# Storing the output rows from SyncE's queue instead of ScalarE's in a fused attention and feed-forward kernel

## The chip, the cores and the metric

One core of one Trainium2 chip runs the whole program. The metric is the device time of one execution in microseconds. A core has a matrix engine (TensorE, PE in the profile), three engines for elementwise work (VectorE, DVE; ScalarE, ACT; GpSimd, POOL) and SyncE (SP), which in this kernel only issues DMAs. ACT and POOL can issue DMAs as well. Each engine takes its own instructions strictly in order.

## The reference

Inputs are q, k, v of shape 4 × 8 × 768 × 64 (batch, head, position, dimension) and the weights of a feed-forward layer. The attention has two kinds of keys under one softmax: the near positions, |i − j| < 16, and 24 summaries of blocks of 32 positions.

```python
k_sum = k.reshape(B, H, nb, block, D).max(axis=3)
v_sum = v.reshape(B, H, nb, block, D).mean(axis=3)
scores_l = scale * q @ k.T                      # kept where |i - j| < 16
scores_s = scale * q @ k_sum.T + log(block)
a = softmax(concat[scores_l, scores_s])
attn = a @ concat[v, v_sum]
x = attn.transpose(0, 2, 1, 3).reshape(3072, 512)
xn = x / sqrt(mean(x * x) + 1e-6) * rms_g
g = xn @ w_gate                                 # 512 -> 1536
out = (g * sigmoid(g) * (xn @ w_val)) @ w_out   # 1536 -> 512
```

The output is 3072 × 512 in float32, 6.29 MB.

## The kernel before, in words

The tokens are cut into 24 units of 128, six per batch. Attention runs unit by unit, all heads together. Units 0 to 5 (batch 0) go through steps whose names begin with su, in float32, and PE transposes their operands. Units 6 to 23 use operands that are split into a high and a low float16 part, and DMA transpositions turn them: kT of the keys (line 729), qT of the queries (`prep_q`, line 796), eT of the exponentials (`expo`, line 858), and, for every unit from 3 on, xT of the normalized attention output (`norm_b`, line 1111). All DMA transpositions are issued by SP; so are all loads.

The block summaries of batches 1 to 3 are made from pieces, hn, of k (the maximum, on DVE, line 682) and of v (the sum, on POOL, line 682). There are eight pieces of each per batch, loaded at line 666 into two buffers; ACT takes sums of squares of them (line 676), the folded results go to memory (`sum`, line 693), and `sum_scale` (line 699) lets PE add the squares up. `load_ks` (line 715) reads the summaries of k back as kr; `split_ks` (line 723) splits them on ACT into khl, which SP transposes into ksT (line 729).

Meanwhile the weights are loaded by SP in pieces of 1 MB (w_gate and w_val at line 554, w_out at line 560), decoded and split: lines 542 to 590 for w_gate and w_val into w_gv, lines 611 to 649 for w_out, where `row_o` (line 627) takes row sums on ACT.

The feed-forward layer runs over nine groups of tokens, of 384, 128, 256 and then six times 384. For each group and each of 12 slices f of the 1536 columns, `gate_val` (line 1258) multiplies xT with the slices of w_gate and w_val, and ACT and DVE form the product h (lines 1267 to 1270); for groups 5 to 8 `seven` (line 1190) does part of it with fewer products. `project` (line 1292) multiplies h with the slice of w_out and accumulates in three PSUM banks, acc, one for each 128 tokens. After the last slice ACT evicts each bank into a tile ob with two buffers (line 1297; the very last tile of the program uses another one, x), and the tile is stored as 256 KB (lines 1298 and 1299). There are 24 such stores. With `qout="a"` ACT's queue issues them, otherwise SP's.

The steps are written in one long list, which fixes the data flow. The order in which each engine issues its instructions is a second thing: a table, ORDER, holds for PE, ACT, DVE, POOL and SP a list of jumps over the instructions as the list produced them, and every engine follows its list. The tables also say where in its queue an engine meets a store or a transposition, and so what waits behind it.

Of the kernel before, what the change touches and what calls it, by code (L numbers as in the profile page):

```python
# [35 lines left out]
    e32a="a", e32b="v", ee="a", fill1="v", fill2="p", hh="a", hh0="a", hl="v", k32="a", ob="v", q32="a", qout="a",  # L36
# [114 lines left out]
0x22 36x2 -38x18 20 -21x8 13 -14x10 8x4 -7 -2 2 -2 13 4x2 -15x4 1 1 -4 1 27x3 -22 -7x2 5 20x2 1 -2 2x2 -23x2 -6x4 23  # L151
-34 33x4 -37 11x2 6 -7 -4 3x2 12 7 -21x3 18x8 -25 27 55 -48 47 -48 -14x3 1x8 2x4 43 1 12 -59 2 55 -16 1 13x3 -62x2 20
23 15x4 -56 -8 8 -2 -8x5 57x5 13 -14x4 -52 -15 75x6 -78 6 -7x2 5 -6x4 27 -17x6 -13x6 79x3 -75 -8 24 -8 63x6 -62 -8x6
-17x2 35x5 11x10 -21x2 19 -20x2 34x9 -25x7 18x6 6x4 8x7 30 -31 -16x2 -12 26 -27 24 29x4 -48 15x2 -28x4 54 -48x5 43 26x2
-28x2 33x2 -9x7 2x2 -37 11 -47x2 11x2 -13x3 10 -11x6 36 23 1x2 -3 -57 -6x2 4x8 10x6 7 -8 7 -8x3 5 -6 53 18 -19 -50x3
21x2 10 -11 23x2 -25 24x2 -51 53 3 -58x2 48x2 -28 27 -28 32 -5 -53 72 -50x2 36x2 -33x3 -8 7 -8x3 23 3 1x2 -3 -5 19
-11x3 8 -9x3 6 -7 -36x7 29x2 4x3 32x4 8x4 -12 -37x2 46 -12x2 -34x3 1 -8 36x2 -33 1 38 -9x2 22x2 -56x2 -10 9x2 35 -36x4
58 -59 31 -32 22 -18 -6 34 -5 4x3 -33 32 -39x2 43 -7x4 13 -26 -30x2 2 50 -51x3 36 -15 14 19 -10 -11x3 17 -36 -52 117x4
-35x4 3x2 10 -11x3 -8 -23 7 -8 7 -8x2 6x4 39 1 -2 1 -34 33x2 -35 5 -17 44x3 -47 15x2 5x3 -8x4 4x8 20 -8x2 6x2 -8x2 6 -7
6x4 -10 13x6 55 -56x4 9 -10 -24 23x4 47 -43x2 -26 25 -8 1x2 -3 14x4 -12x5 7 -8 7x2 -9x2 7x3 -44x3 63x4 6 -7x3 4x5 7 -17  # L160
8x2 -10 9 28x2 -71 40 -40x2 67 -68 1 -2 40 -40 -7 45 -6 5 -41 5 57 -64 34 -35x4 17 -17x4 24 -25 29 7 -8x5 26 -9 19x3
-41x2 1x5 11 21 -22 6 -7 6 -7x2 5 16 -17 -7 6x2 -8 7 64 -91 90x2 -92 24 66x6 -97x2 35x4 -16 15x12 -51 94 -45x7 -57 28
1x2 -3 78x8 16 -39x2 -74 73 36 -37x3 34x2 -36x4 32 -33 32x6 -38 37 -121 92x5 -15 14 -15 14x3 19x8 -27x7 20 3x2 -5 4x2
-104x5 99x4 -102x4 98 15 23x4 -54 10x5 58 -59 10x3 -13x2 -18 52x3 -38 10x2 -12 36x4 -29x2 -13x2 11x2 -129 115 12 24x13
-37 -14 13 -14 -114x2 2x2 -4x2 2x12 145 23 -24 23 -24 23x2 20x11 -56 55x2 -97x2 38 -39x5 34 55 -56 55x3 -94x4 32x3 62x2
-9x5 -60x2 16 45 -63 62 -63 62 -63 14x2 -16 15 -16 60 -46x2 44x2 17 -18x2 -65 64 15 -16x2 14x14 -79x6 30 -31x3 70x8 -36
-68 52 -53 23 -24 23x2 -25 24x2 -26 63x10 -73 313x8 16x19 -35x16 -265 283x5 6x6 -268 2 -3x2 1 1 -2 262x3 -264x2 3 -4 3
-22x8 10 4x2 -3 -4 5x2 3 -4 3 13 -18 3 -4 3 14x2 -4 -5x2 3 -4 5 228 -223 -7 2 3 -4 -4 3 -4 5x2 2 2 -3x2 1 -7x2 5 3 2
-42x2 37 -36 -3 2x2 -4 3 34 -8x2 6 -7 2 205 -200 -4 5 -6 5 -4 -3 5 -4 46 -4 5x2 -7 2 -3 5 -4 3 2 2x2 -7 2 3 -7 -52 4
-5x4 1x3 1 -2 1 3 -4 41 3 5 -4x2 -4 5 -3 2 -7 12 -61 2 -3 5 49 -54x2 2 -3 2x2 1 -2 1x4 5 -6 5x3 -8x4 4 34 -8x2 2x2 -4 5  # L170
3 2 -7x3 4x2 -5x2 3x20 89x2 -91x6 85 -86 85x2 -87x2 105 -106x2 127 -128 82 -83 102x4 -106x3 123 -124x2 124 -24x2 19x2
-124x3 149 -76x2 -76 75x2 44x2 -46 21 49 -27 -124x2 76x2 20x7 -57 2x3 51x2 43 -3 -68 25x2 93x5 5 -104x4 100x3 -103 -65
# [1167 lines left out]
```

## Time and profile before

| what | value |
|---|---|
| median of 3 runs | 706.21 us (702.89 to 707.88) |
| profiled execution | 708.47 us |
| its span | 706.6 us |
| mean granted clock of PE | 0.988 |
| PE busy | 676.8 us, 96% of the span |
| DVE, ACT, POOL busy | 540.8, 497.3, 221.4 us |
| SP's DMA queue, q1 | 239,172 packets, 84.78 MB |
| ACT's DMA queue, q10 (the stores alone) | 3,456 packets, 6.29 MB |

The profile is of one execution. Times within it count from the span's start. In a list of waits, "A <- B: 3.3, 1, 3.3" says that A waited for B 3.3 us in total, once, the longest 3.3 us. In a timeline an idle time of the engine ahead of an instruction stands in brackets with what ended it. The granted clock is a share of PE's full clock of 2.4 GHz. A row of SPq or ACTq is the issue of a DMA by that engine's sequencer, not its transfer.

### The profile page before, as it was taken

The numbers are of one execution on the slowest core, as the hardware profiler recorded it, in microseconds if no ns is written. First come the engines' busy times: TensorE is split into PE (matmuls) and PEld (weight loads), VectorE is DVE, ScalarE is ACT, GpSimd is POOL, SyncE is SP. The second block draws the span as 40 slices with busy tenths as digits, with TensorE's granted clock in tenths as the row PEclk, the third lists the DMA queues.
The fourth block names the chain that finished last, engine by engine and source line by source line (L and its number), as shares of the span: only waits on it lengthen the run. The fifth ranks groups of instructions, "written<-read, shape, count | busy, mean of one in ns | idle before, by whom it ended". The sixth has DMA issues, their size and how long they took to land.

```text
span 706.6 us, 16113 instructions
## 1 busy us (share of the span) xinstructions
PE 676.8 (96%) x5854; PEld 482.1 (68%) x5854; DVE 540.8 (77%) x1599; ACT 497.3 (70%) x1095; POOL 221.4 (31%) x321
## 2 busy tenths in 40 slices
PE   6998999887999999999999999999999999999997
PEld 4686666774556765655655566777988788878874
DVE  3898897766878865766999989999888877675542
ACT  3696785579988678747778687677888778834433
POOL 5564132450333344423125444251233213410000
PEclk9998999988999999999999999999999999999999
DMA  9999645455569698694677774563768444320001
GB/s 192 312 283 289 209 158 123 86 111 118 104 143 154 142 195 161 147 176 100 97 149 183 138 156 109 101 129 72 147 116 160 102 99 84 76 53 19 29 1 60
DMA packets 243859, 93.32 MB, mean 132 GB/s; under 512 B 227716, under 2 KB 227716, under 8 KB 243780
## 3 DMA queue, kind: packets, MB, share of 16 engines
q1 hardware_dynamic: 239172, 84.78, 56.3%
q10 hardware_dynamic: 3456, 6.29, 2.5%
q0 software_dynamic: 1152, 1.22, 0.8%
q8 instruction: 46, 0.75, 0.4%
q14 instruction: 33, 0.27, 0.1%
HBM read 50.45 MB, written 6.59 MB: 81 GB/s over the span
## 4 chain that ended last, share of the span: by engine, by line
PE 64%; DMA 12%; DVE 7%; ACT 6%; SPq 5%; issue 4%; POOL 2%; POOLq 0%; ACTq 0%; DVEq 0%
PE acc L1292 20%; PE gv L1190 17%; PE gv L1258 17%; DMA qT<-qs 4%; SPq L745 3%; PE att L834 3%; PE acc L1258 2%; PE att L875 2%; DMA eT<-ee 2%; DMA wo<-in_moe_w_val_dram 1%; DMA wo<-in_moe_w_gate_dram 1%; ACT junk L627 1%; SPq L554 1%; DMA hn<-in_k_dram 1%; POOL ee L436 1%
## 5 line engine op out<-in xcount | busy, mean ns | idle before, releaser
L1292 PE MATMUL acc<-wo,hhl 128*128 128x512 f16 x864 | 230.2, 381 | 0.3 <-ACT ob L1297 0.2
L1258 PE MATMUL gv<-xT,w_gv 128*128 128x384 f16 (+2 forms) x1296 | 218.7, 306 | 8.3 <-DVE th L1270 4.1
L1258 PEld LDWEIGHTS <-w_gv 128*128 128x128 f16 x1584 | 142.3, 99 | 80.4 <-issue 8.2
L1292 PEld LDWEIGHTS <-hhl 128*128 128x128 f16 x864 | 81.3, 98 | 61.8 <-issue 2.1
L436 POOL TENSOR_TENSOR ee<-sm,ee 128x256 f16<-128x256 f32 (+1 forms) x72 | 70.5, 991 | 154.7 <-ACT ee L431 132.0
L1190 PEld LDWEIGHTS <-w_gv 128*128 128x128 f16 x1008 | 87.3, 98 | 12.1 <-issue 1.5
L849 ACT ACTIVATE sm<-sm,mx,c 128x192 f32<-128x192 f32 x144 | 69.8, 537 | 1.9
L1190 PE MATMUL gv<-S,w_gv 128*128 128x192 f16 x504 | 65.7, 246 | 0.0
L1190 PE MATMUL gv<-xT,w_gv 128*128 128x192 f16 x504 | 54.6, 246 | 0.6 <-DVE R L1224 0.5
L838 DVE CUSTOM_DVE_ANT_0 sm<-att,mask 128x192 f32<-128x192 f32 x144 | 44.6, 352 | 9.3 <-PE att L834 6.2
L1190 PEld LDWEIGHTS <-wo 128*128 128x128 f16 x540 | 47.0, 98 | 6.9 <-issue 1.3
L1190 PE MATMUL gv<-xT,wo 128*128 128x192 f16 x360 | 48.5, 246 | 0.6 <-DVE R L1215 0.4
L875 PEld LDWEIGHTS <-eT 128*128 128x128 f16 x720 | 34.9, 97 | 12.5 <-DMA eT<-ee 1.2
L436 POOL TENSOR_TENSOR xs<-x,xs 128x512 f16<-128x512 f32 x21 | 26.1, 1241 | 55.4 <-ACT xs L431 55.4
L1258 PE MATMUL acc<-xT,w_gv 128*128 128x384 f16 (+1 forms) x288 | 43.0, 272 | 0.0
L875 PE MATMUL att<-vv,eT 128*128 128x65 f16 x720 | 42.0, 193 | 1.0 <-DMA eT<-ee 1.0
L834 PE MATMUL att<-kT,qT 128*128 128x192 f16 x288 | 40.9, 246 | 1.4 <-DMA qT<-qs 1.0
L1267 ACT ACTIVATE th<-gv,gains 128x384 f32<-128x384 f32 (+1 forms) x42 | 22.9, 546 | 23.5 <-PE gv L1258 21.8
L1087 POOL TENSOR_TENSOR x_r<-x_r,consts 128x1 f32<-128x1 f32 x24 | 21.1, 879 | 53.5 <-DVE x_r L1086 44.4
L676 ACT ACTIVATE junk<-hn 96x512 uint8<-96x512 f32 x48 | 29.9, 624 | 10.2 <-DMA hn<-in_k_dram 5.2
L431 ACT CAST ee<-sm 128x256 f16<-128x256 f32 (+1 forms) x72 | 34.9, 507 | 1.9 <-DMA eT<-ee 1.2
L1268 DVE SCALAR_TENSOR_TENSOR th<-th,gv 128x384 f32<-128x384 f32 (+1 forms) x42 | 21.5, 511 | 18.9 <-ACT th L1267 18.9
(308 smaller groups left out, 1347.4 us busy)
## 6 DMA issues: line engine op xcount, KB each, us to landing
wo<-in_moe_w_gate_dram SPq DMA_DIRECT2D x6, 1024.0 KB
wo<-in_moe_w_val_dram SPq DMA_DIRECT2D x6, 1024.0 KB
wo<-in_moe_w_out_dram SPq DMA_DIRECT2D x6, 1024.0 KB
out_dram<-ob ACTq DMA_DIRECT2D x23, 256.0 KB
hn<-in_k_dram SPq DMA_DIRECT2D x24, 192.0 KB
hn<-in_v_dram SPq DMA_DIRECT2D x24, 192.0 KB
vr_l<-in_v_dram SPq DMA_DIRECT2D x15, 256.0 KB
qr_l<-in_q_dram SPq DMA_DIRECT2D x15, 256.0 KB
```

Source lines behind the costliest of these rows:

```text
L431: nc.scalar.copy(o, i)
L436: (nc.vector if ENG.get(op, "p") == "v" else nc.gpsimd).tensor_tensor(o, a, b, op=ALU.subtract)
L676: nc.scalar.activation(junk[0:96], y[:, o:o + DM], AF.Square, accum_out=d["ss"][:, j:j + 1])
L834: nc.tensor.matmul(pt[:, j * SC:(j + 1) * SC], lhsT=s["qT"][:, a * H + h, :], rhs=kT[:, h, :], start=(a == 0), stop=(a == 1))
L838: nc.vector.tensor_tensor_reduce(sm[:, i, :], pt[:, j * SC:(j + 1) * SC], mask, 1.0, NEG, op0=ALU.add, op1=ALU.max, accum_out=mx[:, i:i + 1])
L849: nc.scalar.activation(sm[:, i, :], sm[:, i, :], AF.Exp, scale=s["c"][:, 0:1], bias=mx[:, i:i + 1])
L875: nc.tensor.matmul(po[r][:, h // 2, 0:D + 1], lhsT=e, rhs=vv[:, 0:D + 1], start=(n == 0), stop=(n == len(pairs) - 1))
L1190: nc.tensor.matmul(bank[:, i * T2:(i + 1) * T2], lhsT=right(n, wi, c), rhs=left(xi, c), start=start, stop=(i == 1 and c == 1 and wi == 1), ...
L1258: nc.tensor.matmul(pt[:, 0:T], lhsT=w_gv[:, f - f % 2 + i, wi, c, f % 2, :], rhs=x[:, xi, c, 0:T], start=(n == 0), stop=(n == 3 * NC - 1))
L1267: nc.scalar.activation(th, pg[:, 0:T], AF.Tanh, scale=f_sc[:, f - f % 2:f - f % 2 + 1])
L1268: nc.vector.scalar_tensor_tensor(th, th, 1.0, pg[:, 0:T], op0=ALU.add, op1=ALU.mult)
L1292: nc.tensor.matmul(accs[grp][j], lhsT=h[:, js], rhs=wo_hl[f // 2][:, wi, f % 2, :], start=(f == first and n == 0), stop=(f == (first - 1) ...
```

## The change

One letter of the configuration moves the 24 stores from ACT's instruction stream and queue to SP's: ACT has 979 instructions instead of 1003 and SP 406 instead of 382. PE (5709), DVE (1407) and POOL (330) keep theirs. With it the whole table ORDER is replaced, for all five engines; a row of it tells a reader nothing, so only its head is shown. The steps and their code stay as they are.

```diff
 ENG = dict(
-    e32a="a", e32b="v", ee="a", fill1="v", fill2="p", hh="a", hh0="a", hl="v", k32="a", ob="v", q32="a", qout="a",
+    e32a="a", e32b="v", ee="a", fill1="v", fill2="p", hh="a", hh0="a", hl="v", k32="a", ob="v", q32="a", qout="s",
...
 ORDER = dict(
     PE="""
-0x22 36x2 -38x18 20 -21x8 13 -14x10 8x4 -7 -2 2 -2 13 4x2 -15x4 1 1 -4 1 27x3 -22 -7x2 5 20x2 1 -2 2x2 -23x2 -6x4 23
...
```

PE's instructions move by 5.4 places of 5709 on average, DVE's by 4.2 and POOL's by 3.7. Three places show what moves.

The first is SP's queue where the first transposition of xT stands (xT_1297, of unit 3). wo are pieces of w_out, hn pieces of k or v, kr_1755 the summaries of k that are read back. Before:

```order
L560 DMA wo5_1348<-in_moe_w_out_dram 128x2x1024
L666 DMA hn_1373<-in_k_dram 96x512
L666 DMA hn_1378<-in_k_dram 96x512
L560 DMA wo4_1484<-in_moe_w_out_dram 128x2x1024
L666 DMA hn_1382<-in_v_dram 96x512
L693 DMA sum0_1_924<-hn_1210 96x64
L666 DMA hn_1413<-in_v_dram 96x512
L1111 DMA_TRANSPOSE xT_1297<-xs_1298 128x8x128
L715 DMA kr_1755<-sum0_1_924 24x8x64
L666 DMA hn_1514<-in_v_dram 96x512
```

and now:

```order
L666 DMA hn_1378<-in_k_dram 96x512
L560 DMA wo4_1484<-in_moe_w_out_dram 128x2x1024
L1111 DMA_TRANSPOSE xT_1297<-xs_1298 128x8x128
L745 DMA v2r_2053<-in_v_dram 24x4x64
L666 DMA hn_1382<-in_v_dram 96x512
L693 DMA sum0_1_924<-hn_1210 96x64
L745 DMA vv_141<-in_v_dram 24x4x64
L666 DMA hn_1413<-in_v_dram 96x512
L715 DMA kr_1755<-sum0_1_924 24x8x64
L560 DMA wo5_1348<-in_moe_w_out_dram 128x2x1024
L666 DMA hn_1514<-in_v_dram 96x512
```

The transposition now stands directly behind wo4_1484 and ahead of the two v pieces. The read of kr_1755 keeps its place behind hn_1413, with no transposition ahead of it, and wo5_1348 has come from ahead of both to behind kr_1755.

The second is SP's queue where the stores of the first groups come. ob_2846 is the one tile of group 1 and ob_2751 the third of group 0, eT and qT are transpositions, v2r_l, qr_l and kr_l are loads for attention. Before:

```order
L858 DMA_TRANSPOSE eT_3086<-ee_3077 128x12x128
L693 DMA sum0_2_2067<-hn_2068 96x64
L666 DMA hn_3006<-in_k_dram 96x512
L1111 DMA_TRANSPOSE xT_3060<-xs_3061 128x8x128
L666 DMA hn_3008<-in_k_dram 96x512
L768 DMA v2r_l_2967<-sum1_1_1381 24x4x64
L858 DMA_TRANSPOSE eT_3232<-ee_3223 128x12x128
L666 DMA hn_3234<-in_k_dram 96x512
L796 DMA_TRANSPOSE qT_3157<-qs_3152 128x16x128
```

and now:

```order
L1111 DMA_TRANSPOSE xT_3060<-xs_3061 128x8x128
L1299 DMA out_0_dram<-ob_2846 128x512
L858 DMA_TRANSPOSE eT_3086<-ee_3077 128x12x128
L666 DMA hn_3006<-in_k_dram 96x512
L693 DMA sum0_2_2067<-hn_2068 96x64
L745 DMA v2r_l_3533<-in_v_dram 16x4x64
L745 DMA qr_l_3531<-in_q_dram 128x8x64
L745 DMA kr_l_2963<-in_k_dram 128x8x64
L666 DMA hn_3008<-in_k_dram 96x512
L1299 DMA out_0_dram<-ob_2751 128x512
L768 DMA v2r_l_2967<-sum1_1_1381 24x4x64
L858 DMA_TRANSPOSE eT_3232<-ee_3223 128x12x128
```

Each of the two stores now stands in SP's queue ahead of an eT transposition, one directly and one with a small load between. About 11 of the 24 stores have a transposition in one of the next two rows.

The third is ACT's queue at the evictions of group 0, ob_2739, ob_2745 and ob_2751. Before, the first was followed by its store, and the other two came 24 rows later, here behind work of the next group (hhl, ee) and ahead of a copy for v (vv):

```order
L431 CAST ee_2990<-sm_2756 128x2x2x64
L431 CAST ee_2990<-sm_2756 128x4x128
L431 CAST hhl_2878<-th_2874 128x256
L1297 ACTIVATE ob_2745<-acc_2389,scales_2098 128x512
L1297 ACTIVATE ob_2751<-acc_2390,scales_2098 128x512
L815 ACTIVATE vv_141<-v2r_2311,kv1_s_2148 64x4x64
```

and now:

```order
L1297 ACTIVATE ob_2739<-acc_2388,scales_2098 128x512
L723 ACTIVATE khl_3001<-kr_2568,kv0_s_1646 128x8x64
L1279 ACTIVATE hhl_2780<-h1_227,scales_2098 128x128
L1297 ACTIVATE ob_2745<-acc_2389,scales_2098 128x512
L1279 ACTIVATE hhl_2786<-h1_227,scales_2098 128x128
L815 ACTIVATE vv_141<-v2r_2311,kv1_s_2148 64x4x64
L1279 ACTIVATE hhl_2792<-h1_227,scales_2098 128x128
L1279 ACTIVATE hhl_2798<-h1_227,scales_2098 128x128
L1084 ACTIVATE junk_2690,x_ss_2689<-x_2574 128x512
L1279 ACTIVATE hhl_2804<-h1_227,scales_2098 128x128
L1297 ACTIVATE ob_2751<-acc_2390,scales_2098 128x512
```

The three evictions now stand within eleven rows, and their stores are no longer in this queue.

## Rows read from the trace of the kernel before

**Rows 1.** The page: busy us of each engine (share of span), instructions.

```profile
PE 676.8 (96%) x5854; PEld 482.1 (68%) x5854; DVE 540.8 (77%) x1599; ACT 497.3 (70%) x1095; POOL 221.4 (31%) x321
```

**Rows 2.** Windows by stage: stretch, length, busy us by engine, clock, DMA share, GB/s.

```profile
55.40:171.40 116.00, 104.70 (x908) 78.36 (x909) 90.51 (x259) 83.21 (x170) 37.64 (x61) 0.93 0.56 153
171.40:660.00 488.60, 482.11 (x4248) 338.49 (x4247) 392.48 (x1166) 362.36 (x835) 153.25 (x187) 1.00 0.62 122
```

**Rows 3.** Windows, the three stretches at half clock.

```profile
55.40:62.20 6.80, 6.20 (x48) 5.49 (x49) 5.17 (x12) 4.02 (x9) 3.57 (x8) 0.50 1.08 347
154.30:161.20 6.90, 6.55 (x31) 4.72 (x32) 4.64 (x12) 6.59 (x20) 3.15 (x4) 0.51 0.27 59
168.00:171.40 3.40, 3.40 (x12) 1.55 (x11) 3.40 (x9) 3.35 (x8) 0.00 (x0) 0.50 1.06 205
```

**Rows 4.** PE's waits from 100 to 175 us: total, times, longest.

```profile
PE att L699 <- ACT junk L676: 3.3, 1, 3.3
PE gv L1258 <- DVE th L1270: 2.7, 1, 2.7
PE gv L1258 <- DMA xT<-xs: 2.2, 1, 2.2
```

**Rows 5.** PE's waits in the whole run.

```profile
PE att L576 <- ACT w_gv L570: 3.3, 2, 3.0
...
PE att L834 <- DMA qT<-qs: 1.0, 3, 0.4
PE att L875 <- DMA eT<-ee: 1.0, 2, 0.6
```

**Rows 6.** SP's issues from 100 to 128 us: start, duration, engine, line, transfer.

```profile
104.72 5.46 SPq L666 DMA_DIRECT2D hn<-in_k_dram  x2
110.23 0.42 SPq L560 DMA_DIRECT2D wo<-in_moe_w_out_dram  x1
...
118.46 1.34 SPq L1111 DMA_TRANSPOSE xT<-xs  x1
119.92 0.47 SPq L715 DMA_DIRECT2D kr<-sum  x1
```

**Rows 7.** POOL's timeline, the instruction that completes the transposition's input.

```profile
109.20 1.61 POOL L436 TENSOR_TENSOR xs<-x,xs 128x512 f16<-128x512 f32 x1
```

**Rows 8.** ACT's timeline at 124.86 us.

```profile
124.86 0.72 ACT L723 ACTIVATE khl<-kr,kv_s 32x512 f16<-32x512 f32 x1 [3.04 <-DMA kr<-sum]
```

**Rows 9.** The chain of waits from 100 to 175 us: start, duration, what.

```profile
109.86 3.18 DMA hn<-in_k_dram
...
119.92 4.92 DMA kr<-sum
...
150.83 2.74 DMA hn<-in_v_dram
```

**Rows 10.** Line 1299, the stores: issue ns min/median/max, first and last start.

```profile
L1299 ACTq DMA_DIRECT2D out_dram<-ob x23: 338/339/375, 197.4 to 703.6; - x23
```

**Rows 11.** SP's timeline, one load of 256 KB.

```profile
205.47 0.40 SPq L745 DMA_DIRECT2D qr_l<-in_q_dram  x1
```

**Rows 12.** ACT's timeline from 208 to 251 us, evictions and a store.

```profile
209.13 1.25 ACT L1297 ACTIVATE ob<-acc,scales 128x512 f32<-128x512 f32 x2
...
240.39 0.34 ACTq L1299 DMA_DIRECT2D out_dram<-ob  x1
...
250.32 0.67 ACT L1297 ACTIVATE ob<-acc,scales 128x512 f32<-128x512 f32 x1
```

**Rows 13.** SP's timeline, one transposition.

```profile
349.79 2.93 SPq L796 DMA_TRANSPOSE qT<-qs  x1
```

**Rows 14.** PE's timeline, its reader.

```profile
354.51 0.50 PE L834 MATMUL att<-kT,qT 128*128 128x192 f16 x4
```

**Rows 15.** SP's own waits in the whole run.

```profile
SPq L858 <- POOL ee L436: 45.4, 16, 10.1
```

**Rows 16.** ACT's timeline, the last store.

```profile
703.59 0.34 ACTq L1299 DMA_DIRECT2D out_dram<-ob  x1
```

More of the change, by code (lines that the diff above doesn't have):

```diff
@@ L156 @@
[L156 to L160, printed above, removed]
@@ new lines @@
+9x2 14 -15x2 -13 43x2 -11x3 8x2 -10x5 5x3 -8 7 31x2 10x2 -130x3 127x2 -14 13 -44x2 2 -3x2 26x2 28 -55 25 -26x2 24
+-120x2 80 37x2 25 -53x2 4 46 -52x2 31 -32x2 -10 39 -10x2 8 -9 8 24 -76 18 4 29x7 -36 35 14 -15 -43x2 29 -30 43 -44 2x3
+48 -49 22 25 8x2 7x2 -45 66x2 -33x2 31x2 -57x2 -68 77 -11 28x3 -99 88 -12 -11x3 8x4 23 -17 -20 50 1 -2 1 -35 -9 8x2
+32x3 -57 26 7x3 -10x2 -18 17x4 4 18x2 7 -8x2 6x5 -11x3 8 66 -67 -35x7 18 13x5 -18 18x2 11 -12x7 47x3 -69 18 1 -2 1 -22
+22x2 -17 16x3 6x3 -9x3 6x2 -8x2 -32x2 73 -44 5 28x4 5x4 -9 8x2 6x2 -8 -11 10 -45 72 -40 39 -69x4 35 -36 40 -51x3 7x2 33
@@ new lines @@
+-29 -15x2 42 -36x3 59 -60 35 -36 17 61x2 -80x4 53 22 -39 -15 -25 29x8 16 7 -8x2 -18x6 89 -78 5x2 -7x2 17 4 -23 4x2
+-22x2 36 -17 16 50 -68x3 -24x2 87 -88 87 -53x10 43 -44x3 -27 -11 36x2 -22 1x2 -3 59x9 -76 85x4 -62 47x5 -52x5 47 8x22
+-30x4 26x18 -129 132x8 -108x5 91 11 15 -119x4 162 -25 -52x2 26x4 -20 63 -64x9 30x7 -37x2 53 -19x2 -29x2 27 -154 153
+-29x3 26 14 -77 76 -43 -14x2 38x6 -32 -13 43x5 -162x2 2 -3 2 -3 2x12 149 43x10 -34x3 45 -15x4 -99x10 32 -33 99x3 -70 55
+-89 32 19 -20x2 53x2 11x7 -18x2 -57x5 13x3 -16 67x3 -55 65x11 -22x3 -73 72 -73x2 48x5 -40x6 52 17x9 -79x3 76x2 -100
@@ new lines @@
+-50 22 50 -74 22 -103 79x4 19 -103x2 101 -102x3 48 68 -19x5 -53x2 51x7 -58 93 2 -3 -38x3 88 -154x2 152x4 5x3 -93 28
+-29x6 -48 133x2 5x5 5x5 -108 -48 -5 4 46x7 70x2 -60 59x3 -133 137x5 5x5 -152 3 52 99x5 -157 66x3 -68 67x4 -21x8 13x2
+-73 72 -73 72x4 -80 158 -80x11 65 -65 -2 1x12 55 61x3 2 -71 3 -4 66x2 1 3 -4 -125x4 53 2x2 66 -60 55 -122x6 60x3 -11
+-53 55 62 -4 5x2 -4 3x2 -5 -74 14x8 55 -56x7 49x3 2 -3x2 5 -5 4 -5x3 2x8 -64x2 -7 6x8 -14x4 10x8 -52 3x3 91x5 -95x2
+93x3 -54x6 48 89 -79x22 57 2x2 -4 3 -94x2 88 3 -97 3 -4 31x2 6x3 77 -78x15 -51x2 -5 59x2 -8 -54 60x3 -10x3 -53 -4 55 6
@@ new lines @@
+-51 80x3 5x2 -4x2 5 -4x3 1x3 -99 1 -7x2 101 9x4 8 -9 8 -9x5 4x2 -6x2 37 -34 -26 25x7 26 1x4 -162 129x5 7 -8 7 -8 20
+-21x3 4 -5 4 -5 4x8 -54 -3 2 1x2 -3 2 -7 65 -4 3 4 11 -12x4 8 -9x5 4 42x2 2 -52x2 62 -13x2 -5 -63 17x7 137 -138x2 -26
+-7 40x3 28 -20 14 -25x3 7x2 -9 8 -53 163x2 2x2 -4 -170 55 -51 166 -4 5 -130 9 -21 -7 145x3 -142 -7 15 9 -10x2 8 -9
+-18x2 3 134 5 -6 10 -6 -122x4 118 4 -5 4 -5x2 3x3 -156 159x3 -117x8 102x3 -105x5 104 -5 4x6 -131 2 27x9 -20 19x2 -21 20
+-21x9 24 -98 38 58x6 -19x12 7x5 -66 -4 3 64x9 3x7 -10 9x5 -14x2 -80 131 2 22x4 8 -21x3 9x3 6 -167 130 -131 158x4 3 -4
@@ L309 @@
+-3 -3 -6 -3 9 -3 4 -2 -22 22 5x2 -5 -3 2 -3 9 -5x2 5 -3 -4 5 -6 -7 8 6x2 -5x3 3 -8 7 1 2x2 -6 1 -6 5 3x3 3 -8 7 -5 4 -5
+4 -5 4x2 3x2 -5x3 2
 """,
     Pool="""
[L311 to L313 removed]
@@ L330 @@
+-4 1 17 7 -13x2 -4 -3 -3x2 -3 20x2 -28 29 -16 12 -4 -17 -6 26x2 -14 15 -7 7 -4 -14 1 -2 -6x2 1 15 -4 4 1 -2 1 1x2 -3 4
+-3x2
 """,
```

312 lines of the change are left out of this document (147 added, 165 removed).

## The prediction

> **What bounds the kernel now.** I read four views, from the widest to the narrowest. The page shows that the matmuls of TensorE (PE) are busy 676.8 of 706.6 us and no other engine is above 541 [rows 1]. So PE is the bound, and only what makes PE idle or slow can move the time. The windows by stage show where PE is not busy: 11.3 us (116.0 less 104.7) between 55 and 171 us, where the granted clock is 0.93, but 6.5 us (488.6 less 482.1) in the long middle from 171 to 660 us [rows 2]. The middle, where nearly all output stores lie, has little left to give and much to lose; the stage before it has gaps worth naming. PE's waits there name them: 3.3 us on ScalarE's (ACT's) sum of squares, 2.7 us on VectorE's th, 2.2 us on the DMA transposition of xT [rows 4]. The last view is the granted clock: three stretches of 6.8, 6.9 and 3.4 us ran at half clock (1.2 of 2.4 GHz) [rows 3]. They follow gaps of PE of 3.0 us (on w_gv, line 570 [rows 5]), of 3.3 and of 2.7 us [rows 4]; the gap of 2.2 us was followed by none.
>
> **The scale.** The profiled execution took 708.47 us, of which its span is 706.6; it is 2.26 above the median of the runs, 706.21. I make the sum against 708.47 and take 2.26 off at the end.
>
> **Part 1, the first transposition of xT moves forward on SyncE (SP).** SP issues in order. Before, xT's transposition is issued at 118.46 [rows 6], though its input is complete at 110.81 (109.20 + 1.61) [rows 7]: it stands behind loads of v pieces, and each of those waits for a buffer. In the new order it stands right behind the 1 MB load of w_out that was issued at 110.23 [rows 6], ahead of the v pieces, so it can be issued at about 111, 7.5 us earlier. PE wants it at 122.4 (its wait ends at 124.6 after 2.2 us), and from 111 the same transposition needs 6.1 us (124.6 less 118.46), so it lands near 117 and the wait of 2.2 us goes [rows 4]. The load of kr from the block sums was issued at 119.92, just behind that transposition, and took 4.92 us on the chain [rows 9]; ACT stood idle 3.04 us for it [rows 8]. With no transposition ahead of it I expect it at about 118.5, and landing in 3.0 to 3.5 us, as the loads beside it in the chain did (3.18 and 2.74 [rows 9]): ACT's khl then starts near 122, 2.4 to 3.0 us earlier. That matters because the chain runs on from khl to the v piece at 150.83 [rows 9] and from there to PE's wait of 3.3 us on ACT [rows 4]; were only PE's 2.2 us gone and this chain left where it is, PE would wait so much longer there. Both move, so I count −2.2. Bounds: 0 (the chain stays, the wait grows) and −3.0 (ACT's whole wait goes).
>
> **Part 2, 24 stores leave ACT.** Each cost ACT's sequencer 0.34 us [rows 10]: 24 × 0.34 = 8.1 us. ACT is busy 497 of 707 us and PE waits for it nearly nowhere in the middle, so the gain is 0; bounds 0 and −1.0, a little of the idle 6.5 us of [rows 2].
>
> **Part 3, 24 stores come to SP.** A load of the same 256 KB costs SP 0.40 us [rows 11], a store cost ACT 0.34: 24 × 0.34 to 0.40 = 8.1 to 9.6 us of issue. SP has room on the whole: in one of its waits alone it stood 45.4 us for inputs of transpositions [rows 15]. What counts is a transposition behind a store. In the new order about 11 of the 24 stores stand directly, or one row, ahead of a transposition that PE will read. The tightest such transposition of before was issued at 349.79 and its issue took 2.93, to 352.72; PE's reader began at 354.51 [rows 13, 14], so it has at most 1.8 us of slack. A delay by the issue of 0.34 to 0.40 is hidden by it. Where the store also waits for its eviction on ACT, it holds the queue. But the stores were loose before: two tiles were evicted from 209.13 on, a store of that group was issued at 240.39, and the next group's first eviction came at 250.32, with no wait of PE [rows 12]; in the new order the three evictions of group 0 stand close together and their stores behind them. No row of before shows a store in SP's ring, so its price there I bound. From below: nothing, since the transfers of store and transposition used the same DMA engines before. From above: the last store was issued from 703.59 to 703.93 and the span ended at 706.6 [rows 16], so a store takes at most 2.7 us after its issue; the transposition behind it may be late by that, 2.7 less 1.8 of slack = 0.9 us, in 11 places = 9.9 us. I take 0, the end that is nearer to the row at which PE waits for transpositions now: three waits of 1.0 us together for qT, two of 1.0 for eT, out of 18 and 36 transpositions [rows 5], in a queue that already carries loads of 256 KB just ahead of them.
>
> On the ring the Trainium skill has two rules, and they disagree on this change. *DMA: Bandwidth & Descriptors*, section "Issuing engines are not separate DMA queues", says that transfers from any issuing engine run on the same 16 DMA engines and interleave, and that another issuing engine only saves issue time; by that the ring costs 0. The section "Queues, rings and completion order" there says that each DMA engine takes turns between the queue rows that have work, packet by packet; by that a store in its own row took turns with a transposition, and in SP's row it goes wholly first, which would be the +9.9 above. The trace of before bears out neither, since its stores never shared SP's row.
>
> **Part 4, the rest.** The first 55 us carry the same loads in another order, and the gap behind w_gv keeps its ACT sequence: 0, bounds 0 and +1.0 (two issues of a load and the wait of one piece). The last store's issue goes from ACT, directly behind the eviction, to SP, which has nothing else to do then: +0.1, bounds 0 and +0.5. The reordered matmuls, and the vector instructions that move by a few places, move no group's end by more than some tenths: 0.
>
> **Sum.** −2.2 + 0 + 0 + 0 + 0.1 = −2.1: 706.4 on the scale of the profiled execution; less 2.26 that is 704.1, and I say 704.
>
> **The rivals.**
> *A, slower: transpositions behind stores.* As priced in part 3: +9.9 − 2.1 gives 714. For it: SP takes its work in order, and a wait there blocks all that follows; PE's slack at the tightest place is 1.8 us. Against it: most transpositions have more slack than the tightest, and PE waited for only five of them. It decides where store and hold-up together exceed 1.8 us.
> *B, faster: the stretch before 171 us gains more.* Behind the v piece of 150.83 come ACT's sums, then the rows of w_out, then PE. If freed buffers let that piece be loaded a round trip earlier (2.74 us [rows 9] and the wait for its buffer, 4 to 5 us together), everything behind it moves by that: 706.2 − 2.1 − 4 to 5 = 699 to 700. If PE's wait of 2.7 us [rows 4] shrinks as well, the half clock behind it goes too (3.4 us at half speed [rows 3], worth 1.7): 697 to 698. I price B at 698. Against it: nothing in the new order loads that piece earlier than its buffers allow.
> *C, nothing.* The transposition comes earlier and PE simply waits longer for ACT at line 699: the 2.2 us stay, 706.
>
> **How the numbers follow.** Forecast 0.52, A 0.19, B 0.18, C 0.11. A change of 1% is 7.1 us (below 699.1, above 713.3), about what can be told from no change. A lies at the upper bound, mostly above it: slower 0.19, with some from a startup that goes wrong and less from a milder A. B lies around the lower bound: faster 0.18 and a little from the forecast's own spread. The forecast's own range is 702 (−3.0 and −1.0) to 707 (0 and +1.0); to leave out no more than 2 in 10 it must reach into both rivals: 697 to 714. So faster 0.20, same 0.61, slower 0.19.
>
> **What would show it.** Right: PE has no wait on xT near 122, ACT's khl starts near 122, PE's wait at line 699 stays near 3 us with the half-clock stretch behind it, the waits on qT and eT stay near 1 us each, and SP's stores issue in 0.34 to 0.40. Wrong by A: the waits on qT and eT sum to 5 us or more, each behind a store, and PE's idle time from 171 to 660 us grows above 6.5. Wrong by B: no half clock near 155. Wrong by C: a wait near 5.5 us at line 699.

## The result, and the profile after

The changed kernel took 710.85 us (median of 9 runs, 708.44 to 712.41) against 706.21 (9 runs): a ratio of 1.0069, 95% interval 1.0043 to 1.0095. Two later series of the same kernel, each beside its own runs of before, gave 1.0052 [1.0023, 1.0080] and 1.0038 [1.0011, 1.0066]; one execution of the last series (716.65 us) was in the slower state and is left out. The changed kernel is about half a per cent slower, 3 to 5 us; 704 was forecast. Its profiled execution took 709.88 us with a span of 708.1.

PE's busy time and the windows by stage, which answer to [rows 1] and [rows 2]:

```profile
PE 674.9 (95%) x5854; PEld 481.5 (68%) x5854; DVE 545.5 (77%) x1599; ACT 498.9 (70%) x1095; POOL 215.9 (30%) x321
```

```profile
55.40:171.40 116.00, 103.95 (x897) 77.78 (x897) 91.31 (x254) 82.41 (x167) 39.02 (x61) 0.93 0.57 155
171.40:660.00 488.60, 480.34 (x4232) 337.06 (x4231) 395.25 (x1165) 363.58 (x835) 149.13 (x187) 1.00 0.60 121
```

PE idles 12.1 us between 55 and 171 us (11.3 before) and 8.3 us from 171 to 660 (6.5 before): the middle, of which I had written that there is much to lose, lost. PE's waits from 100 to 175 us (total, times, longest), beside [rows 4]:

```profile
PE gv L1258 <- DVE h L1270: 3.4, 2, 1.8
PE gv L1258 <- DVE th L1270: 2.7, 1, 2.7
PE att L1065 <- ACT eT L431: 2.4, 1, 2.4
PE att L699 <- ACT junk L676: 2.1, 1, 2.1
```

The wait on xT is gone, as forecast, and a wait of 2.4 us on ACT's copy eT has come. From 171 us on, beside [rows 5], with the row of POOL that shows what the third wait was for:

```profile
PE att L875 <- DMA eT<-ee: 3.2, 4, 1.3
PE att L834 <- DMA qT<-qs: 1.8, 1, 1.8
PE att L834 <- POOL kT L433: 0.8, 1, 0.8
```

```profile
502.42 0.29 POOL L433 COPY kT<-kT 128x128 f16<-128x128 f16 x1 [6.50 <-DMA kT<-khl]
```

The kT for which PE waited is copied by POOL, and POOL had waited for SP's transposition. That is 5.8 us on transposed tiles in place of 2.0. SP's issues (start, duration, transfer) beside [rows 6], and the piece of k in the chain beside [rows 9]:

```profile
105.30 0.43 SPq L560 DMA_DIRECT2D wo<-in_moe_w_out_dram  x1
...
107.13 0.32 SPq L666 DMA_DIRECT2D hn<-in_k_dram  x1
107.50 0.43 SPq L560 DMA_DIRECT2D wo<-in_moe_w_out_dram  x1
108.03 2.16 SPq L1111 DMA_TRANSPOSE xT<-xs  x1
...
118.46 0.39 SPq L715 DMA_DIRECT2D kr<-sum  x1
```

```profile
107.13 6.49 DMA hn<-in_k_dram
```

The transposition is issued 10 us earlier than before, but the piece of k took 6.49 us, where the one of before took 3.18. ACT's khl, beside [rows 8], begins at 123.98, only 0.9 us earlier, and ACT no longer idles ahead of it; it has other work:

```profile
123.98 0.70 ACT L723 ACTIVATE khl<-kr,kv_s 32x512 f16<-32x512 f32 x1
```

The half-clock stretches, beside [rows 3], are 6.8, 3.4, 3.4 and 3.4 us, 17.0 together (17.1 before); the one at 116.8 is new and follows PE's idle time at line 1065:

```profile
116.80:120.20 3.40, 3.40 (x18) 3.17 (x16) 2.80 (x14) 1.36 (x2) 0.00 (x0) 0.50 0.39 89
```

The stores on SP, beside [rows 10], take 0.42 us of issue in the median and up to 0.93. The qT and its reader, beside [rows 13, 14], now at the place with the longest wait, with the nearest store ahead of it and the two rows directly ahead:

```profile
L1299 SPq DMA_DIRECT2D out_dram<-ob x23: 332/420/927, 197.4 to 705.1; - x23
```

```profile
316.05 0.42 SPq L1299 DMA_DIRECT2D out_dram<-ob  x1
...
325.19 1.24 SPq L729 DMA_TRANSPOSE kT<-khl  x1
326.47 0.59 SPq L745 DMA_DIRECT2D kr_l<-in_k_dram  x1
327.17 3.00 SPq L796 DMA_TRANSPOSE qT<-qs  x1
```

```profile
331.30 0.38 PE L1292 MATMUL acc<-wo,hhl 128*128 128x512 f16 x1
333.50 0.34 PE L834 MATMUL att<-kT,qT 128*128 128x192 f16 x2 [1.83 <-DMA qT<-qs]
```

The four waits of this size on transposed tiles, near 213, 331, 502 and 551 us, are followed through the experiments. None of the four tiles is issued directly behind a store: the nearest one ahead was issued 6.8, 11.1, 22.9 and 22.2 us earlier. SP's rows for the first, the third and the last of them:

```profile
203.70 0.86 SPq L1299 DMA_DIRECT2D out_dram<-ob  x1
...
210.52 1.44 SPq L858 DMA_TRANSPOSE eT<-ee  x1
```

```profile
475.54 0.58 SPq L1299 DMA_DIRECT2D out_dram<-ob  x1
...
498.42 2.01 SPq L729 DMA_TRANSPOSE kT<-khl  x1
```

```profile
526.09 0.37 SPq L1299 DMA_DIRECT2D out_dram<-ob  x1
...
548.28 1.43 SPq L858 DMA_TRANSPOSE eT<-ee  x1
```

A measure for the late part. Executions of one kernel differ by several microseconds, and much of that arises before 171 us: the half-clock stretch near 56 us, for one, lasted 6.8 us in the first profile of before and 10.2 in a second. So beside the timed ratios I use the time from the first matmul of line 834 (scores of unit 6) to PE's last matmul, each read from PE's timeline. Here it is 173.18 to 704.32 (701.78 + 2.54), 531.1 us; before it was 173.09 to 702.84, 529.8. These rows are from after:

```profile
173.18 0.82 PE L834 MATMUL att<-kT,qT 128*128 128x192 f16 x8
...
701.78 2.54 PE L1292 MATMUL acc<-wo,hhl 128*128 128x512 f16 x11
```

### The profile page after: what moved, and what is told of

Read it like the earlier page. It is cut to its first block, busy times and chain, and to the rows that moved or that the text cites. A ratio compares the mean times of both kernels' runs of the same rounds, so it can differ in the third digit from the quotient of the medians.

```text
span 708.1 us, 16142 instructions
## 1 busy us (share of the span) xinstructions
PE 674.9 (95%) x5854; PEld 481.5 (68%) x5854; DVE 545.5 (77%) x1599; ACT 498.9 (70%) x1095; POOL 215.9 (30%) x321
## 4 chain that ended last, share of the span: by engine, by line
PE 63%; DVE 9%; ACT 8%; DMA 8%; issue 5%; SPq 4%; POOL 2%; ACTq 0%; DVEq 0%; POOLq 0%
PE acc L1292 19%; PE gv L1190 16%; PE gv L1258 15%; PE acc L1258 3%; DMA eT<-ee 3%; SPq L745 3%; PE att L875 2%; PE att L834 2%; DMA hn<-in_k_dram 1%; ACT sm L849 1%; ACT junk L627 1%; DVE sm L838 1%; POOL ee L436 1%; PE att L1026 1%; DMA v1f<-in_v_dram 1%
## 5 line engine op out<-in xcount | busy, mean ns | idle before, releaser
L1292 PE MATMUL acc<-wo,hhl 128*128 128x512 f16 x864 | 233.8, 381 | 0.0
L1190 PE MATMUL gv<-S,w_gv 128*128 128x192 f16 x504 | 64.2, 246 | 0.1
L875 PE MATMUL att<-vv,eT 128*128 128x65 f16 x720 | 43.7, 193 | 3.5 <-DMA eT<-ee 3.2
L834 PEld LDWEIGHTS <-qT 128*128 128x128 f16 x288 | 26.0, 98 | 14.7 <-DMA qT<-qs 2.8
L682 POOL TENSOR_TENSOR hn<-hn 96x512 f32<-96x512 f32 x18 | 24.2, 1342 | 35.8 <-DMA hn<-in_v_dram 20.6
```

What stands on the lines that cost most here:

```text
L682: eng.tensor_tensor(x[:, 0:w], x[:, 0:w], y[:, 0:w], op=op)
L834: nc.tensor.matmul(pt[:, j * SC:(j + 1) * SC], lhsT=s["qT"][:, a * H + h, :], rhs=kT[:, h, :], start=(a == 0), stop=(a == 1))
L875: nc.tensor.matmul(po[r][:, h // 2, 0:D + 1], lhsT=e, rhs=vv[:, 0:D + 1], start=(n == 0), stop=(n == len(pairs) - 1))
L1190: nc.tensor.matmul(bank[:, i * T2:(i + 1) * T2], lhsT=right(n, wi, c), rhs=left(xi, c), start=start, stop=(i == 1 and c == 1 and wi == 1), ...
L1292: nc.tensor.matmul(accs[grp][j], lhsT=h[:, js], rhs=wo_hl[f // 2][:, wi, f % 2, :], start=(f == first and n == 0), stop=(f == (first - 1) ...
```

## The experiments

Theory Q: stores in SP's queue hold up the transpositions behind them (the prediction's rival A). Theory O: the queue is free, and the new order of the instructions costs the time. All versions below have 12 timed executions in each series (the version with stores back on ACT 6), beside 23 to 35 of before on the same chip. "Late part" is the measure above.

| version | ratio to before | 95% interval | late part, us |
|---|---|---|---|
| before, again | 1.0004 | 0.9981 to 1.0027 | 530.4 |
| before, stores on SP | 1.0010 | 0.9991 to 1.0030 | 530.2 |
| before, xT moved | 0.9995 | 0.9971 to 1.0020 | 528.9 |
| order of after to 171 us, then before | 1.0006 | 0.9975 to 1.0037 | 530.0 |
| order of after to 95 us, then before | 0.9996 | 0.9971 to 1.0021 | 532.8 |
| before, two scores earlier on PE | 1.0028 | 1.0002 to 1.0053 | 532.0 |
| after, second and third series | 1.0052, 1.0038 | 1.0023 to 1.0080, 1.0011 to 1.0066 | 533.1, 532.7 |
| order of before to 171 us, then after | 1.0011 | 0.9985 to 1.0036 | 531.3 |
| after, stores on ACT | 1.0098 | 1.0070 to 1.0126 | 532.8 |
| after, two SP moves undone | 1.0066 | 1.0039 to 1.0093 | 536.9 |
| after, w_out load behind the piece of k | 1.0018 | 0.9989 to 1.0046 | 533.4 |
| after, PE's four places put back | 0.9998, 1.0014 | 0.9968 to 1.0027, 0.9989 to 1.0039 | 531.2, 530.2 |
| after, two of them (scores) | 1.0044, 1.0023 | 1.0013 to 1.0075, 0.9994 to 1.0051 | 529.6, 530.0 |
| after, the other two | 1.0029 | 1.0001 to 1.0058 | 533.6 |
| after, four places and w_out load | 1.0009 | 0.9980 to 1.0037 | 529.4 |

**1. The queue alone.** In the order of before, only the stores change their queue (SP's rows; one of 24):

```diff
 L745 DMA v2r<-in_v_dram 24x4x64
+L1299 DMA out_dram<-ob 128x512
 L796 DMA_TRANSPOSE qT<-qs 128x16x128
```

> Every engine keeps its order of before; only the 24 stores leave ACT's queue for SP's, each at the place in SP's order where SP stood when ACT issued the store before. Theory Q (stores in SP's queue hold up the transpositions behind them, and that is what the change costs): 709 to 712 us, with waits of PE on qT and eT of 4 us or more in place of 2.0. Theory O (the new order of SP's loads and transpositions costs it, the queue itself is free): 704 to 707 us, waits on qT and eT near 2.

1.0010. That is against Q: stores stand directly ahead of qT here too, and the time stays. PE's waits on qT and eT are 2.3 and 1.3 us, against 1.0 and 1.0 in before. That the stores delay these transpositions is not shown, for with the stores on ACT and the late order of before (experiment 3) the two waits were 3.2 and 0.5. The late part is that of before (530.2 against 529.8 and 530.4). The issues were dearer than forecast, 0.55 us in the median; SP has the room.

**2. The order with the stores back on ACT**, one of 24:

```diff
 L1297 ACTIVATE ob<-acc,scales 128x512
 L1279 ACTIVATE hhl<-h_227,scales 128x128
 L815 ACTIVATE vv<-v2r,kv_s 64x4x64
+L1299 DMA out_dram<-ob 128x512
```

> Every engine keeps its order of after; only the 24 stores go back to ACT's queue, two instructions behind their evictions. Theory Q: 704 to 707 us, the late eT near 213 us and the late qT near 331 us are gone. Theory O: 709 to 712 us, both are still late and so is ACT's copy near 112 us.

1.0098, slower than both theories had it (714.84 us against 712 at most). The order costs without the stores in SP's queue: against Q. Two waits shrank (eT near 213 us from 1.3 to 0.8, qT near 331 from 1.8 to 0.6), two stayed (0.8 and 1.2 near 502 and 551). Why it is slower even than after is open. In its profile 2.8 us lie ahead of the first matmul of line 834 (175.96 against 173.18), where no store has been issued yet, and about 1.7 us in the tail, which lasted 5.5 us from PE's last matmul to the end, against 3.8 in before and after. What else the stores cost ACT when they stand so near their evictions was not followed up.

**3. The two halves.** What was issued before 171 us has one kernel's order, the rest the other's; no row is new.

```diff
 each engine, instructions issued before 171 us: order of after
-each engine, the rest: order of after, stores on SP
+each engine, the rest: order of before, stores on ACT
```

> What every engine issued before 171 us in the profile of after keeps the order of after, the rest has the order of before, and all 24 stores (all of them later than 171 us) are in ACT's queue. If the loss lies in the new order ahead of 171 us (the transposition of xT that slows the piece of k beside it): 709 to 712 us. If it lies behind 171 us, in stores or order: 703 to 707 us.

1.0006, and the reverse,

```diff
-each engine, instructions issued before 171 us: order of after
+each engine, instructions issued before 171 us: order of before
 each engine, the rest: order of after, stores on SP
```

> The other half of the split at 171 us: what every engine issued before 171 us in the profile of before keeps the order of before, the rest has the order of after with all 24 stores in SP's queue. If the late order costs the time: 709 to 711 us, with the waits near 213, 331 and 551 us. If the loss needs the early order: 706 to 708 us.

1.0011. Neither half alone has a loss that its interval separates from none; the sum, 0.17%, lies below the whole's 0.38 to 0.69. The traces are sharper: with the late order of after all four waits were there again (1.7, 1.3, 0.9 and 1.1 us), with that of before none of the four. That profile has a wait of 2.2 us on another qT, near 260, where the first profile of before has 0.4; its late part is 530.0 all the same, so a wait does not always add its length.

**4. Before once more.** No edit.

> The kernel before, unchanged: 703 to 708 us, ratio 1.000 within its interval. What its profile tells is which of the waits of PE and which half-clock stretches of the first profile of before come back in another execution; by both theories the waits on qT and eT stay at about 2 us together.

As expected in time. The profile corrects the prediction: PE does not wait for the first transposition of xT, for which it waited 2.2 us in the first profile. The 0.4 us in this list belong to a later transposition of xT, read at 155.43:

```profile
PE att L699 <- ACT junk L676: 3.8, 1, 3.8
PE gv L1258 <- DVE th L1270: 2.7, 1, 2.7
PE att L637 <- DVE tmp L635: 2.4, 1, 2.4
PE gv L1258 <- DMA xT<-xs: 0.4, 1, 0.4
```

```profile
123.42 1.30 PE L1258 MATMUL acc<-xT,w_gv 128*128 128x384 f16 x7
124.56 0.22 PE L1258 MATMUL gv<-xT,w_gv 128*128 128x128 f16 x1
...
155.43 6.51 PE L1258 MATMUL gv<-xT,w_gv 128*128 128x256 f16 x43 [0.43 <-DMA xT<-xs]
```

PE came to the first place 2.3 us later here, after a half-clock stretch of 10.2 us, so the row that I had counted as −2.2 was the slack that an earlier arrival of PE had opened. Of the five profiles with the order of before ahead of 171 us and xT in its old place, only the first has this wait.

```profile
56.40:66.60 10.20, 9.70 (x62) 7.17 (x63) 7.52 (x20) 6.66 (x10) 5.23 (x17) 0.50 1.08 304
```

**5. The move of xT alone, in the kernel before** (SP):

```diff
 L560 DMA wo_1484<-in_moe_w_out_dram 128x2x1024
+L1111 DMA_TRANSPOSE xT<-xs 128x8x128
 L666 DMA hn<-in_v_dram 96x512
 L693 DMA sum_1_924<-hn 96x64
 L666 DMA hn<-in_v_dram 96x512
-L1111 DMA_TRANSPOSE xT<-xs 128x8x128
```

> The kernel before with one move: the first transposition of xT stands in SP's queue directly behind the 1 MB load issued at 110.2 us, ahead of the two v pieces, as in the kernel after. The prediction's step 1: the wait of 2.2 us on xT goes, 2 us faster, 704 to 706 us against 706 to 708. Theory H (the transposition slows the piece of k that was issued just ahead of it, and the chain goes through that piece): the piece takes 5 to 6.5 us in place of 3.2, PE waits 2 to 2.5 us at line 1065 near 112 us in place of the wait on xT, and the time is that of before within 1 us.

0.9995: the prediction's part 1 gives nothing in time. Theory H was wrong as well: no wait at line 1065 came, and ACT read the piece 3.0 us after its issue had ended (109.34 to 112.33), as in before (2.9).

**6. The load ahead of the piece of k, in the kernel after** (SP):

```diff
-L560 DMA wo_1273<-in_moe_w_out_dram 128x2x1024
 L745 DMA hhl<-in_v_dram 24x4x64
 L666 DMA hn<-in_k_dram 96x512
+L560 DMA wo_1273<-in_moe_w_out_dram 128x2x1024
 L560 DMA wo_1484<-in_moe_w_out_dram 128x2x1024
 L1111 DMA_TRANSPOSE xT<-xs 128x8x128
```

> The kernel after with one move in SP's queue: the 1 MB load of w_out that was issued at 105.3 us, ahead of the piece of k issued at 107.1, goes behind that piece. If the load ahead slowed the piece (6.5 us in place of 3.2): the piece takes 3 to 4 us, PE's wait near 112 us at line 1065 (2.4 us) shrinks to under 1, no half-clock stretch starts near 117, and the time falls by 1 to 3 us. If the transposition of xT behind the piece slowed it: no change.

The piece, issued at 107.23, is read by ACT at 110.91 with no wait ahead, so it took at most 3.7 us; PE's wait at line 1065 and the half clock near 117 are gone. The transposition still follows, issued 1.4 us behind the piece (0.9 in after). Both are gone as well in the profile of experiment 12 that has this edit. The wait is not the same in every execution of after: the piece took 6.5, 5.0 and 6.3 us in its three profiles and PE waited 2.4, 1.0 and 2.2; in one profile of experiment 11, with the load ahead too, the piece took 3.8 and no wait came. Together with experiment 5 this speaks for the 1 MB load ahead as what slowed the piece, and against the transposition behind it.

```profile
110.91 0.61 ACT L676 ACTIVATE junk<-hn 96x512 uint8<-96x512 f32 x1
```

The time came to 1.0018 [0.9989, 1.0046], below the three of the kernel after but with overlap. A later wait grew: PE waited 4.7 us in three pieces for h of line 1270, against 3.4 in two.

**7. Two moves in SP's queue undone, in the kernel after**, the first:

```diff
-L729 DMA_TRANSPOSE kT<-khl 128x8x128
-L745 DMA kr_l<-in_k_dram 128x8x64
 L796 DMA_TRANSPOSE qT<-qs 128x16x128
+L729 DMA_TRANSPOSE kT<-khl 128x8x128
+L745 DMA kr_l<-in_k_dram 128x8x64
```

> The kernel after with two moves in SP's queue alone undone: the qT near 327 us goes ahead of the kT and the 256 KB load that had come ahead of it, and the eT near 548 us goes ahead of the xT and five small loads that had come ahead of it. The stores stay where they are. If the order of transpositions in SP's queue makes PE wait: the wait of 1.8 us near 331 and that of 1.0 near 551 go, and the stretch from 320 to 560 us is 2 to 3 us shorter than in the kernel after beside it (707 to 709 us). If the stores in the queue do it: no change.

Missed: 1.0066, no gain. The waits near 331 and 551 went, as foretold, but others took their place. PE waited 2.3 us on an eT near 287, with a half-clock stretch behind it, which lengthened the late part. And ahead of 334.61 ACT stood still for 3.8 us. ACT's khl must wait until kT has been read by its transposition, and in the order of after it stands early on ACT, ahead of th, on which PE then waits. From ACT's and PE's timelines:

```profile
334.61 0.72 ACT L723 ACTIVATE khl<-kr_l,kv_s 128x512 f16<-128x512 f32 x1 [3.78 <-DMA kT<-khl]
```

```profile
338.73 0.48 PE L1258 MATMUL gv<-xT,w_gv 128*128 128x384 f16 x2 [1.33 <-DVE th L1268]
```

So SP's order at this place cannot be undone by itself; ACT's order needs it. That turned me to the reader: theory P, that PE's own new order reads the tile too early.

**8. The kernel after, second series.** No edit.

> The kernel after, unchanged, beside the next three: 709 to 712 us, +0.4 to +0.7% over before, and in its profile again PE's waits on the eT near 213 and 551 us and the qT near 331 us (1.3, 1.0 and 1.8 us in the first profile). If these three waits are not there, they were of one execution only and explain nothing.

All four waits came again, 1.5 and 1.7 us near 211 and 330, 0.8 and 1.0 near 502 and 551: they belong to the kernel. A third series:

> The kernel after, unchanged, beside the next three on one chip: 0.5 to 0.7% over before.

1.0038, less than foretold; the four again, 1.6, 1.0, 0.8 and 0.9.

**9. PE's order put back at the four places.** The largest of them, by runs of equal steps on PE (gate matmuls of slice 0, projections, scores of unit 13):

```diff
-13 gate, 1 projection, 2 scores, 1 gate, 1 score, 3 gate, ..., 3 gate, 3 projections, 5 gate, 5 scores
+1 projection, 4 gate, 3 projections, 16 gate, 8 scores
```

> The kernel after; in PE's order alone, the matmuls of four short places (where PE waited near 213, 331, 502 and 551 us) are put back into the relative order that they have in the kernel before. SP's order and the stores are those of after. Theory P (the new order of PE reads two transposed tiles earlier than SP can have them: the scores of unit 13 by some 20 gate matmuls, those of unit 19 by some 21): the waits near 331 (1.3 to 1.8 us) and 502 (0.8) go, those near 213 and 551, where PE's reader moved by 0 to 3 places, stay, and the stretch from 180 us to the end is 2 to 2.5 us shorter than in the kernel after. Theory S (SP's order and stores alone make the tiles late): all four stay.

0.9998. By the order itself the first score had been put ahead of 7 gate matmuls and 3 projections there, and that of unit 19 ahead of 5 projections and 21 products of line 1190 (the expectation's "some 20" was wrong for the first). At 0.16 us a gate matmul (16 of them from 328.89 to 331.49 in the rows of experiment 11) and 0.22 a projection, the ten are 1.8 us: as much as the wait of 1.83 in the first profile of after (1.7 and 1.0 in the others). The wait near 331 is down to 0.2 us and that near 502 is gone; the one near 213 is halved (0.65), the one near 551 stays (1.1). The late part is 531.2, not 2 us below the 531.1 of the first profile of after; once, PE waited 1.0 us for DVE's q_i, which no other profile has. Once more:

> The version with all four places put back, once more: the time of before within 0.25% if the first result (ratio 0.9998) stands; 0.4% over before or more if that was chance.

1.0014, late part 530.2. Both series lie below all three of the kernel after, though single intervals overlap. Weighted by their intervals, the three of after give 1.0054 [1.0038, 1.0069] and these two 1.0007 [0.9988, 1.0026]. Nothing but PE's order at the four places differs.

**10. The inverse, in the kernel before**: the same two scores moved ahead, nothing else. At the place of unit 13:

```diff
-1 projection, 4 gate, 3 projections, 16 gate, 8 scores
+13 gate, 1 projection, 2 scores, 1 gate, 1 score, 3 gate, ..., 3 gate, 3 projections, 5 gate, 5 scores
```

> The inverse: the kernel before, stores on ACT; in PE's order alone, the matmuls around the scores of units 13 and 19 get the relative order of the kernel after. Theory P: PE now waits 0.5 to 2 us near 333 and up to 1 us near 503, where before it waited nowhere, and the stretch from 180 us on is 1 to 2 us longer. Theory S: no wait.

1.0028 [1.0002, 1.0053], late part 532.0 against 528.9 to 530.4. The wait near 502 is made:

```profile
499.85 0.25 PE L1190 MATMUL gv<-xT,wo 128*128 128x192 f16 x1
501.45 0.26 PE L834 MATMUL att<-kT,qT 128*128 128x192 f16 x1 [1.36 <-DMA qT<-qs]
```

The one near 333 did not show as a gap of PE, so there P foretold too much. SP's issue and PE's reader at that place:

```profile
324.59 1.97 SPq L796 DMA_TRANSPOSE qT<-qs  x1
```

```profile
326.80 2.93 PE L1258 MATMUL gv<-xT,w_gv 128*128 128x384 f16 x17
329.56 0.33 PE L834 MATMUL att<-kT,qT 128*128 128x192 f16 x2
```

The reader came 5.0 us after the qT's issue began and did not wait; in after it got the tile only 6.3 us after that (327.17 to 333.50). In before, as here, the qT stands ahead of a kT, in after behind a kT and a load of 256 KB. So PE's earlier reader does not make the wait near 331 alone. It takes SP's new order too, and experiment 7, which undid SP's part, took this wait away as experiment 9 did. Near 502 the tile differs: here PE waits for the qT, in after for the kT.

**11. Two of the places, and the other two.** The scores of units 13 and 19 only:

> The kernel after; PE's order is put back at two of the four places only, the scores of units 13 and 19. Theory P: the waits near 331 and 502 us are gone, those near 213 and 551 stay (1.3 to 2.0 and 1.0 to 1.5 us), and the time is 2 us below that of the kernel after, 707 to 710 us, no more than 0.3% over before. If the gain of the version with four places came from chance or from the other two places: 710 to 713 us, 0.5% or more over before.

> The version with the scores of units 13 and 19 put back, once more. Theory P (these two places are the larger part of the loss): 0.1 to 0.4% over before, 1 to 3 us below the kernel after beside it. If its loss of the first time stands at 0.5% or more, the two waits that its profile no longer has were not what costs the time.

Their edit is that of experiment 9 at two places. In the trace it does what P says: PE runs into the scores of unit 13 without a gap, and the late part is 529.6 and 530.0, that of before.

```profile
328.89 2.76 PE L1258 MATMUL gv<-xT,w_gv 128*128 128x384 f16 x16
331.49 0.82 PE L834 MATMUL att<-kT,qT 128*128 128x192 f16 x8
```

In time the two series gave 1.0044, more than P allowed (0.3%), and 1.0023, within it. So it is not shown that these two places are the larger part of the loss. The complement:

> The complement: the kernel after with PE's order put back only at the other two places (the second half of unit 7's attention near 213 us and of unit 20's near 551 us). Theory P: waits near 331 (1.3 to 1.8 us) and 502 (0.8) are there, 0.4 to 0.6% over before. If these places matter instead: at most 0.2% over before.

1.0029, between what the two theories said, and the late part is 533.6, that of after; its trace has the waits on the scores:

```profile
PE att L834 <- DMA qT<-qs: 1.9, 1, 1.9
...
PE att L834 <- POOL kT L433: 0.9, 1, 0.9
```

**12. Looking for a faster version.** Near 60 us PE's matmuls ran up to 1.9 us earlier in the profile of after than the same ones in before (the first of line 987 at 59.61 against 61.55). That start, with the rest of before:

```diff
 each engine, instructions issued before 95 us: order of after
-each engine, the rest: order of after
+each engine, the rest: order of before
```

> What every engine issued before 95 us in the profile of after has the order of after, all the rest the order of before, stores on ACT. At 90 us the profiles with the order of after stood 1.9 us earlier on average than those with the order of before. If that holds to the end, this kernel is 1 to 2 us faster than before (705 to 707 against 707 to 708.5). If the wait of PE on ACT's sums near 150 us takes it back: no difference.

0.9996: the start's gain does not reach the end. This execution also had a half-clock stretch at 258.8 us, behind a wait of 2.11 us on qT, which lengthened its late part. And the edits of 6 and 9 together:

> Two edits that each lowered the time of the kernel after, together: PE's order put back at the four places, and the 1 MB load of w_out behind the piece of k. If the losses are separate: 705 to 707 us, 0.1 to 0.4% below before. If the second place only shifts the wait (PE was held by h near 140 us in both): the time of before, within 1 us.

1.0009 [0.9980, 1.0037], late part 529.4: no gain over before. No version here is faster than before beyond its interval.

## Why the prediction was wrong

**The step that failed** is the last of part 4: the reordered matmuls "move no group's end by more than some tenths: 0". The runs showed in its place that PE's order at four short places costs most of the loss: put back, they bring the ratio from 1.0054 to 1.0007, and put into before, two of them cost 0.28% [0.02, 0.53]. The late part, without the profiles that hold a half-clock stretch in it, is 528.9 to 530.4 us in the five with PE's late order of before. It is 531.1 to 533.6 in the five with the early scores and the stores on SP, 529.6 and 530.0 with the scores of units 13 and 19 put back, and 531.2 and 530.2 with all four places. I looked at where each group's matmuls end, a mean of 5.4 places, and not at which moved matmul reads a tile that comes from SP. The other moved matmuls kept their new places in experiment 9 and cost nothing clear of noise; the first score of unit 13, ten matmuls earlier and with its qT later in SP's queue, waited 1.0 to 1.8 us in the three profiles of after.

The slack of 1.8 us in part 3 was misread too. PE already waited for five transpositions of before [rows 5], so the tightest had no slack at all. And 1.8 is counted from the end of the issue [rows 13, 14], while the qT near 331 in after reached its reader 3.3 us after its issue had ended (330.17 to 333.50).

**Part 1** (−2.2) failed by its row. The wait on xT did go, but it stood in one profile of before and not in the other; the move alone gave 0.9995. And the chain did not move as said: kr was issued at 118.46, as forecast, but khl began 0.9 us earlier, not 2.4 to 3.0, behind an activation of h that had waited for PE until 122.80 (120.29 in before), while a piece of k behind a 1 MB load took 3.3 us longer (6.49 against 3.18), with a wait of 2.4 us behind it (1.0 and 2.2 in the two later profiles). I had followed xT and kr in SP's new order, not the load that had come to stand ahead of the piece.

**Parts 2 and 3** came out right in their sum: the 24 stores on SP gave 1.0010 [0.9991, 1.0030] in the order of before, though the median issue took 0.42 and 0.55 us, not 0.34 to 0.40. Of the two rules of the Trainium skill that I set against each other (*DMA: Bandwidth & Descriptors*), the one of "Issuing engines are not separate DMA queues" is what this run agrees with. The price of 9.9 us that I had worked out beside the other did not appear; how the DMA engines take turns was not tested. The start (0, bounds 0 and +1.0) was up to 1.9 us early instead, and that did not reach the end.

**The rivals.** Two of rival A's signs came (waits on transposed tiles of 5.8 us, PE's idle time in the middle 8.3), the third did not: none of the four late tiles stands directly behind a store. The same waits stand with the stores on ACT, two of them smaller. At one of these, the eT near 213, SP issues almost without a break from the store on, so a share of some 0.5 us may be the store's (1.3 against 0.8). A was not the cause of the whole: the stores alone, in the order of before, cost nothing clear of noise. B did not come: a half-clock stretch stands near 158. C did not either: the wait at line 699 was 2.1 us, not 5.5.

**Open**: how much of the whole lies ahead of 171 us. The halves of experiment 3 give 0.06% and 0.11%, the whole 0.38 to 0.69; the late half has all four waits and yet no loss clear of none. The load of experiment 6 may have a part. And the split among the four places is open: the traces show which waits go with which place, but the timed intervals of two, the other two and all four overlap, and the two scores put back, with the late part of before, still gave 1.0044 once.

## What to carry to other kernels

When an order table changes, list the instructions that read what a DMA delivers. See how many places each of them has moved on its engine, and how the issue of that DMA has moved on its own; a mean displacement says nothing about either. A wait of PE in one profile is worth its length only if a second execution has it too: here a wait of 2.2 us was gone in the second. And undo a moved transfer only together with what stands behind it on the other engines: putting qT ahead of kT freed PE and stopped ACT.

## What was not expected of the hardware

The half-clock stretch near 56 us was 6.8 us in one execution of the kernel before and 10.2 in another, behind the same gap of PE on w_gv (3.0 and 2.7 us): an estimated 1.7 us of difference by itself (half of the 3.4 us). The issue of one and the same transposition, xT of unit 3, took 1.34 us of SP's time in before, 1.67 to 2.16 in the three profiles of after and 3.95 in experiment 6, where it stood directly behind two loads of 1 MB.
